# One function set on ScalarE, a scaling of the value weights, and a new share-out of the opening's PSUM copies in an FFT-plus-channel-mix kernel

## The chip, the cores and the metric

The kernel runs on 1 core of one Trainium2 chip. The metric is the device time of one execution in microseconds (us). The core's engines are TensorE (PE in the profile, with its weight loads as PEld), VectorE (DVE), ScalarE (ACT), GpSimd (POOL) and SyncE (SP). Each engine works through its own list of instructions in the order in which they were recorded; semaphores order the engines against each other.

## The reference

```python
X = fft(fft(x, axis=1), axis=2).real               # x: 8 x 3072 x 256, float32
x_prev = X shifted by one along the sequence, zeros first
xk = mu_k * X + (1 - mu_k) * x_prev
xr = mu_r * X + (1 - mu_r) * x_prev
k  = max(xk @ w_k, 0)                              # w_k: 256 x 1024
v  = (k * k) @ w_v                                 # w_v: 1024 x 256
r  = 1 / (1 + exp(-(xr @ w_r)))                    # w_r: 256 x 256
out = r * v
```

## The kernel before, in words

The program is one straight list, written out in Python; the order of the recording calls is the order on every engine, and it is pinned. It has an **opening**, in which tables are made and the transform of batch 0 is worked out in pieces, and then a loop over 192 steps (8 batches x 6 chunks of 512 positions x 4 steps).

PSUM holds three wide buffers of 1024 columns (`ps_w()`, psW) and two of 512 (`ps_v()`, psV), each given out in turn. A buffer that is given out again waits for the engines that read it before. Where ScalarE and VectorE both read one buffer, the program also keeps the two one behind the other.

The transform of a batch has three stages on TensorE. Stage one (`a_sum`, L681) multiplies the folded input `p` (made on VectorE by `fold`, L172 and L174) with `w_pm`; its result is copied to `a`. Stage two (`d_units`, L703) makes 13 units of 256 columns, copied to `g_all` by `d_evac`; `d_small` is the same for one or two units in a psV buffer. One column of each unit is then turned by a small product (`turned`, L752). Stage three (`c_sums`, L771) sums `f = 0` and `f = 1` parts into "slots" of 128 columns; they are copied to `y`. All these copies go through `evac`: ScalarE at L574, VectorE at L572.

The mix makes `x` from `y`: `diff` (L854) takes differences `d`, `scaled` (L866) multiplies with mu, `mixed` (L877) adds. The first four slots of batch 0 are mixed apart, by `ts` (L308: any tensor-scalar operation) and a scalar_tensor_tensor at L1049 that reads its other operand from the PSUM buffer named `first`.

A step of the loop (`k_piece`) multiplies `x` with a quarter of `w_k` into a psW buffer (L912), and ScalarE takes the relu of it into `rl` (L922), with a scale of 0.25. `square` (L932) squares a piece on VectorE. The value products (`v_part`, L965, for the first chunks, `v_tile`, L953, later) follow three to five steps behind. `r_item` makes the products with `w_r` (L939) and the sigmoid (L944), and `v_out` (L975) multiplies value and sigmoid on VectorE and writes the result out.

What a step does besides is in a table: `at(step, f, ...)` puts a call into a step, either among the TensorE products ("x") or behind them ("w"); `event(step, ...)` puts it between the two. Within a step the order is `k_piece`, "x", value products, "e", "w", the output, and last the square. The first two pieces of the first chunk are multiplied in two halves of 256 columns: the first half belongs to slots 0 to 3 and stands in the opening, the second half in steps 0 and 1.

`keep_busy(n, ps)` (L235) records n products of zeros whose results nobody reads; `NF` holds the counts by place. Names with a number behind them (psW_360, x_388) are buffers by the number of their allocation, which differs between the two programs; `first` is psW_361 in both.

Of the kernel before, what the change touches and what calls it, by code (L numbers as in the profile page):

```python
# [39 lines left out]
def kernel(  # L40
# [37 lines left out]
    def ps_w():  # L78
        return ps_slot("W", 3, 1024)
# [152 lines left out]
    def keep_busy(n, ps, cols=512):  # L232

        for _ in range(n):
            nc.tensor.matmul(out=ps[:, 0:cols], lhsT=zeros,  # L235
                             rhs=_v(zeros, 0, [(0, cols // P), (1, P)]), start=True, stop=True)

    fill = ps_w()
    keep_busy(4, fill)
    NF = (8, 4, 1, 3, 0, 0, 0)  # L240

# [58 lines left out]

    m_cs = const.tile([P, 3, NJ, 64], FP16)
    warm = const.tile([P, 1], FP32)
    nc.scalar.activation(out=warm, in_=zeros[:, 0:1], func=AF.Sin, bias=0.0, scale=1.0)
    def ts(out, in0, s1, op0, s2=None, op1=None):
        kw = {} if op1 is None else {"op1": op1}
        V.tensor_scalar(out=out, in0=in0, scalar1=s1, scalar2=s2, op0=op0, **kw)  # L308
# [360 lines left out]
    def a_sum(b, h, i0, eng="A", m=4):  # L669


        if (h, i0) == (0, 0):
            a_tile(b)
        ps = ps_w() if m == 4 else ps_v()
        for i in range(m):
            parts = [(h, i0 + i + 1 - h, 0, 2 * WA, 0, 1)]
            if h and i0 + i == 7:
                parts = [(0, 0, 0, WA, WA, 1), (1, 7, 1, WA, 1, 2)]
            for half, q, o, n, w, step in parts:
                for k in range(2):  # L680
                    nc.tensor.matmul(out=_v(ps, 256 * i + o, [(2 * WA // n, n)]),  # L681
                                     lhsT=p_t[b, half][0:96, q, 128 * k:128 * k + 128],
                                     rhs=_v(w_pm[0:96], (WA + WB) * k + w,
                                            [(WA + WB, 2), (step, n // 2)]),
                                     start=(k == 0), stop=(k == 1))
        a_ps[b, h, i0] = ps
        if eng:
            a_evac(b, h, i0, eng, m)
# [7 lines left out]
    def d_units(b, ps, u0, n, bank):  # L696

        for i in range(n):  # L700
            for e in range(2):
                o = bank * e + 128 * i
                nc.tensor.matmul(out=ps[:, o:o + 128],  # L703
                                 lhsT=a_t[b][:, e, 2 * (u0 + i):2 * (u0 + i) + 2, :],
                                 rhs=w_eo[:, e], start=True, stop=True)
# [228 lines left out]
    def r_item(c):  # L934
        b, m, i = c
        ps = ps_w()
        for tb in range(4):
            for a in range(2):
                nc.tensor.matmul(out=ps[:, 256 * tb:256 * tb + 256],  # L939
                                 lhsT=x_t[b, 1, m][:, a, 512 * i + 128 * tb:  # L940
                                                   512 * i + 128 * tb + 128],
                                 rhs=wr_sb[m][a], start=(a == 0), stop=(a == 1))
        st["r", c] = o_pool.tile([P, 1024], FP16, name="r", bufs=2)
        nc.scalar.activation(out=st["r", c], in_=ps, func=AF.Sigmoid)  # L944

    def v_tile(c, tb):

# [21 lines left out]
    def v_out(c, tb, n):  # L969
        b, m, i = c  # L970
        o = o_pool.tile([P, 2, 256], FP32, name="o" if n == 2 else f"o{tb}",
                        bufs=4 if n == 2 else 1)
        t0 = tb + 1 - n

        V.scalar_tensor_tensor(out=o.rearrange("p a b -> p (a b)")[:, 0:256 * n],  # L975
                               in0=st["v", t0][:, 0:256 * n], scalar=16.0,
                               in1=st["r", c][:, 256 * t0:256 * (t0 + n)],
                               op0=ALU.mult, op1=ALU.mult)
# [14 lines left out]
    eo_rest()  # L993
    m_sine(0, NJ1)
    m_sine(NJ1, NJ)
    nc.scalar.activation(out=warm, in_=zeros[:, 0:1], func=AF.Sigmoid)
    fold(0, 0, 1, 4)
    mu_ps = ps_v()
    for a in range(2):
# [2 lines left out]
    for n in range(2):  # L1002
        outer(mu_ps[:, 4 + n:5 + n], (tv(TO + n, 0, (1, P)), rv(ONE, 0, (1, 1))))
    keep_busy(NF[1], fill)
    a_sum(0, 0, 0)
    fold(0, 0, 5, 4)
    a_sum(0, 0, 4)
    nc.scalar.activation(out=muf_t, in_=mu_ps[:, 0:6], func=AF.Copy)
    loads()
    keep_busy(NF[2], ang_ps[1])  # L1010
    fold(0, 1, 0, 4)
    a_sum(0, 1, 0, "A")
    fold(0, 1, 4, 4)
# [1 line left out]
    a_sum(0, 1, 4, "V", 2)  # L1015
    a_sum(0, 1, 6, "A", 2)
    turn_table()
    nc.scalar.activation(out=mu_n, in_=mu_f, func=AF.Copy, bias=1.0, scale=-1.0)
    m_neg()
    fill = ps_w()  # L1020
    keep_busy(NF[3], fill)
    small = [ps_v(), ps_v()]
    for u, ps in enumerate(small):
        d_units(0, ps, u, 1, 128)
        d_evac(ps, u, 1, 128, "AV"[u])
    d_units(0, fill, 2, 4, 512)
# [5 lines left out]
    turned(0, 2, small[0][:, 256:258], "V")  # L1032
    ts(g_0[:, 0:1], small[0][:, 256:257], -1.0, MUL)
# [9 lines left out]
    x_t[0, 0, 0] = mix_pool.tile([P, 2, 1536], FP16, name="x00")  # L1043
    for a in range(2):
        t = x_t["t", a] = mix_pool.tile([P, 24, 64], FP16, name=f"t{a}")
        ts(t[:, 0:4], y[:, 0:4, a], mu_n[:, a, 0:1], MUL)
    for a in range(2):
        for z in range(2):
            V.scalar_tensor_tensor(out=_v(x_t[0, 0, 0], 1536 * a + 64 * z, [(128, 2), (1, 64)]),  # L1049
                                   in0=_v(first, 512 + 64 * a - 384 * z, [(128, 2), (1, 64)]),  # L1050
                                   scalar=mu_f[:, a, 0:1],
                                   in1=_v(x_t["t", a], 64 * z, [(128, 2), (1, 64)]),
                                   op0=ALU.mult, op1=ALU.add)
    odd = ps_v()
    even = ps_v()
    for f in range(2):
        c_sums((w[:, 0:512], w[:, 512:1024]), 5, 4, f)
    keep_busy(NF[5], w[:, 768:1024], 256)
    turned(4, 8, fill[:, 0:4])
    c_sums((even, odd), 9, 8, 0)  # L1060
    keep_busy(NF[6], w[:, 768:1024], 256)
    c_sums((even, odd), 9, 8, 1)
    y_evac(0, 5, 4, w)
    for z, p in enumerate((odd, even)):
        evac(_v(y, 128 * (9 + z), [(256, 4), (1, 128)]), p, "A")

    work = {}

# [33 lines left out]
    for a in range(2):  # L1104
        for ds in range(2):
            k_products(chunks[0], ds, 0, 256, (a,))
# [138 lines left out]
    for step in range(nk + LAG):  # L1245
        if step < nk:
            k_piece(chunks[step // 4], step % 4)
        due(step, "x")
        v = v_steps.get(step)
        if v and step not in early_v:  # L1250
            v_tile(*v)
        if step in p_steps and step not in early_v:
            v_part(*p_steps[step])
        due(step, "e")
        if step + 1 in early_v:
            if step + 1 in v_steps:
                v_tile(*v_steps[step + 1])
            if step + 1 in p_steps:
                v_part(*p_steps[step + 1])
        early = step in OUT_FIRST  # L1260
        for v in o_steps.get(step, ()) if early else ():
            v_out(*v)
        due(step, "w")
        for v in () if early else o_steps.get(step, ()):
            v_out(*v)
        if step < 4 * EARLY + 4:
            square(chunks[step // 4], step % 4, 1, step in SQUARE_A)
        elif step < nk and step % 2:
            square(chunks[step // 4], step % 4)
# [32 lines left out]
```

## Time and profile before

| | |
|---|---|
| median of 3 runs | 426.31 us (426.04 to 426.9) |
| the profiled execution | 426.17 us, of which the span from the first to the last instruction is 424.4 us |
| TensorE busy | 418.4 us (99%), 3974 products |
| VectorE busy | 371.3 us (87%) |
| ScalarE busy | 332.4 us (78%) |
| GpSimd busy | 64.2 us (15%) |
| HBM | 32.08 MB read, 25.17 MB written |

In the rows of the trace the first number is the start in us from the first instruction and the second is the duration; "x8" means that eight instructions were merged into one row, whose duration then runs from the first start to the last end. What stands in brackets is the idle time of the engine before it and what ended it. In the groups by shape the columns behind the bar are the busy time in us, the mean of one in ns, and the idle time before them. Instructions of one engine overlap a little in the rows (the next starts some 0.1 us before the last has ended), so a chain of them is added up from start to start.

### The profile page before, as it was taken

What the parts mean: (1) busy time and instruction counts of PE and PEld (TensorE: products, weight loads), DVE (VectorE), ACT (ScalarE), POOL (GpSimd) and SP (SyncE); (2) the same over time, 40 slices, a digit from 0 to 9 for tenths busy, and PEclk for the clock granted to TensorE, in tenths of its full rate; (3) what the DMA queues carried; (4) which work ended last, traced back from release to release, by engine and by line L of the source; (5) the groups of instructions that cost most, each with busy time, mean ns of one, the idle gap of its engine ahead of it and who ended that gap; (6) DMA issues with size and microseconds to landing.
All of it is one profiled execution on the core that took longest, in us unless ns stands there. A gap on an engine that the chain in (4) does not pass through costs nothing.

```text
span 424.4 us, 9646 instructions
## 1 busy us (share of the span) xinstructions
PE 418.4 (99%) x3974; PEld 294.1 (69%) x3974; DVE 371.3 (87%) x593; ACT 332.4 (78%) x438; POOL 64.2 (15%) x99
## 2 busy tenths in 40 slices
PE   8999999999999999999999999999999999999996
PEld 3767766776677767776767776777777776776765
DVE  8899999999898999989999899989999676977553
ACT  7889886798768986699767996689876997666661
POOL 7478500200060001400041000500000000000000
PEclk9999999999999999999999999999999999999999
DMA  8779962632385223932349232772233232332333
GB/s 171 111 111 195 224 156 57 113 91 64 70 151 147 64 59 62 215 101 51 76 77 220 52 75 59 134 174 55 52 76 72 58 73 52 74 74 51 76 76 99
DMA packets 35104, 42.08 MB, mean 99 GB/s; under 512 B 4114, under 2 KB 31092, under 8 KB 35060
## 3 DMA queue, kind: packets, MB, share of 16 engines
q1 hardware_dynamic: 27488, 25.41, 24.4%
q0 software_dynamic: 7264, 15.80, 21.8%
q8 instruction: 31, 0.51, 0.5%
q10 hardware_dynamic: 308, 0.26, 0.2%
q14 instruction: 13, 0.11, 0.1%
HBM read 32.08 MB, written 25.17 MB: 135 GB/s over the span
## 4 chain that ended last, share of the span: by engine, by line
PE 98%; DVE 1%; issue 0%; POOL 0%; ACT 0%; POOLq 0%
PE psW L912 39%; PE psV L953 37%; PE psW L939 10%; PE psV L965 3%; PE psW L611 3%; PE psW L235 1%; PE psV L611 1%; PE psW L681 1%; PE psW L703 1%; PE psV L378 1%; PE psW L771 0%; PE psW L803 0%; DVE rw L308 0%; PE psV L703 0%; PE psW L663 0%
## 5 line engine op out<-in xcount | busy, mean ns | idle before, releaser
L922 ACT ACTIVATE rl<-psW 128x1024 f16<-128x1024 f32 x192 | 194.3, 1039 | 79.2 <-PE psW L912 75.5
L912 PE MATMUL psW<-x,wk 128*128 128x512 f16 (+1 forms) x776 | 194.4, 377 | 0.3 <-DVE x L1049 0.3
L953 PE MATMUL psV<-wv_sb,k 128*128 128x256 f16 x1424 | 184.2, 273 | 0.0
L953 PEld LDWEIGHTS <-k 128*128 128x128 f16 x1424 | 136.8, 98 | 38.9
L932 DVE TENSOR_TENSOR k<-rl 128x2048 f16<-128x2048 f16 (+1 forms) x100 | 115.5, 1156 | 32.9 <-ACT rl L922 32.8
L912 PEld LDWEIGHTS <-wk 128*128 128x128 f16 x776 | 75.7, 98 | 53.7 <-issue 0.4
L975 DVE SCALAR_TENSOR_TENSOR o<-psV,r 128x512 f32<-128x512 f32 (+1 forms) x97 | 65.7, 680 | 10.0 <-PE psV L953 9.0
L877 DVE TENSOR_TENSOR x<-y,t 128x1536 f16<-128x1536 f16 (+3 forms) x76 | 62.4, 827 | 2.2
L944 ACT ACTIVATE r<-psW 128x1024 f16<-128x1024 f32 x48 | 50.0, 1043 | 0.8 <-PE psW L939 0.8
L939 PE MATMUL psW<-wr,x 128*128 128x256 f16 x384 | 49.8, 273 | 0.0
L939 PEld LDWEIGHTS <-x 128*128 128x128 f16 x384 | 37.5, 98 | 14.1
L574 ACT ACTIVATE a<-psW 128x832 f16<-128x832 f32 (+4 forms) x36 | 29.0, 851 | 0.2 <-PE psW L663 0.2
L574 ACT ACTIVATE g_all<-psW 128x512 f16<-128x512 f32 (+5 forms) x47 | 26.7, 646 | 0.3 <-PE psW L703 0.2
L494 POOL IOTA gate<- 1x1 int32 x7 | 0.8, 121 | 163.4 <-DVE gate L493 163.4
L141 POOL DMA_INDIRECT xm<-in_x_dram,idx_g x18 | 23.3, 1294 | 5.5 <-issue 5.5
L866 DVE TENSOR_SCALAR t<-d,muf_t 128x1536 f16<-128x1536 f16 (+3 forms) x44 | 21.9, 508 | 0.1
L172 DVE TENSOR_TENSOR p<-xp,xm 112x2304 f16<-112x2304 f16 (+6 forms) x19 | 21.6, 1139 | 0.0
L574 ACT ACTIVATE pq<-psW 128x1024 f16<-128x1024 f32 (+1 forms) x21 | 20.4, 1007 | 0.1
L866 DVE TENSOR_SCALAR t<-d,mu_m 128x1536 f16<-128x1536 f16 x32 | 19.6, 611 | 0.0
L854 DVE TENSOR_TENSOR d<-y 128x1664 f16<-128x1664 f16 (+5 forms) x19 | 16.7, 879 | 0.3 <-ACT y L574 0.3
L846 DVE TENSOR_TENSOR y<-pq 128x960 f16<-128x960 f16 (+3 forms) x28 | 15.7, 603 | 0.4
L965 PE MATMUL psV<-wv_sb,k 128*128 128x256 f16 x112 | 14.7, 273 | 0.0
(158 smaller groups left out, 236.3 us busy)
## 6 DMA issues: line engine op xcount, KB each, us to landing
out_dram<-o SPq DMA_DIRECT2D x189, 128.0 KB, 2.4
xp<-in_x_dram POOLq DMA_DIRECT2D x12, 216.0 KB, 5.2
xp<-in_x_dram POOLq DMA_DIRECT2D x13, 192.0 KB, 6.8
xp<-in_x_dram POOLq DMA_DIRECT2D x2, 384.0 KB
wv_sb<-in_moe_w_v_dram POOLq DMA_DIRECT2D x1, 512.0 KB
xp<-in_x_dram SPq DMA_DIRECT2D x1, 480.0 KB, 4.3
xp<-in_x_dram POOLq DMA_DIRECT2D x1, 432.0 KB, 4.9
xm<-in_x_dram,idx_g POOLq DMA_INDIRECT x18, 6.9
```

The lines of the kernel that those rows point to most:

```text
L141: nc.gpsimd.indirect_dma_start(dst, None, src, bass.IndirectOffsetOnAxis(ap=idx, axis=0))
L574: nc.scalar.activation(out=out_ap, in_=in_ap, func=AF.Copy)
L866: V.tensor_scalar(out=dst, in0=src, scalar1=mu, scalar2=None, op0=ALU.mult)
L877: V.tensor_tensor(out=_v(x_t[b, j, m], o, [(64 * step, hi - lo), (step, 64)]), in0=y_t[b][:, lo + 3 * m:hi + 3 * m, a], in1=x_t["t", a][:, ...
L912: nc.tensor.matmul(out=st["k", ds][:, 512 * hs + lo:512 * hs + hi], lhsT=wk_sb[m][a][:, 128 * fc:128 * fc + 128], rhs=xk[:, a, 512 * i + l ...
L922: nc.scalar.activation(out=st["rl"][:, 2 * ds:2 * ds + 2], in_=st["k", ds].rearrange("p (f t) -> p f t", f=2), func=AF.Relu, bias=0.0, sca ...
L932: V.tensor_tensor(out=k2_t[c][:, lo:hi], in0=r, in1=r, op=ALU.mult)
L939: nc.tensor.matmul(out=ps[:, 256 * tb:256 * tb + 256], lhsT=x_t[b, 1, m][:, a, 512 * i + 128 * tb: 512 * i + 128 * tb + 128], rhs=wr_sb[m] ...
L944: nc.scalar.activation(out=st["r", c], in_=ps, func=AF.Sigmoid)
L953: nc.tensor.matmul(out=st["v", tb - h][:, 256 * h:256 * h + 256], lhsT=k2_t[c][:, fc, 128 * tb:128 * tb + 128], rhs=wv_sb[:, fc], start=(f ...
L965: nc.tensor.matmul(out=st["v", tb - h][:, 256 * h:256 * h + 256], lhsT=k2_t[c][:, fc, 128 * tb:128 * tb + 128], rhs=wv_sb[:, fc], start=fc ...
L975: V.scalar_tensor_tensor(out=o.rearrange("p a b -> p (a b)")[:, 0:256 * n], in0=st["v", t0][:, 0:256 * n], scalar=16.0, in1=st["r", c][:, ...
```

## The change: what it does

1. **Sigmoid from tanh.** `r` becomes tanh(0.5 z) instead of sigmoid(z), and `v_out` computes (r + 1) * v; the factor 1/2 and the former factor 16 are put into the value weights, which are multiplied by 8 in place, once, by VectorE. `r` is stored in float32 instead of float16. ScalarE loads one function set, at the start; the second load and the dummy activation behind it are gone.
2. **First four slots.** The multiplication with `mu_n`, which read the copied `y`, now reads the PSUM buffer `first`, so those four slots no longer wait for the copy to `y`, and the copy itself comes later.
3. **The opening.** Stage two's units 6 and 7 go into the second halves of the two psV buffers instead of a psW buffer; stage three is summed for slots 0 to 3 and 4 to 8 instead of 0 to 4 and 5 to 8; its last part (`c_sums((even, odd), 9, 8, 1)`) comes behind the first two products with `w_k`. The copies are shared out anew between ScalarE and VectorE. Three places with zero products remain, with 8, 2 and 2 of them (before: 8, 4, 1 and 3). The copies of mu to `muf_t` and `mu_n` come ahead of stage one's.
4. **The first square** comes ahead of the rest of step 0, and the scaling of the value weights right behind it.

The diff, cut to these:

```diff
-    NF = (8, 4, 1, 3, 0, 0, 0)
+    NF = (8, 2, 2)
...
-    nc.scalar.activation(out=warm, in_=zeros[:, 0:1], func=AF.Sin, bias=0.0, scale=1.0)
+    nc.scalar.activation(out=warm, in_=zeros[:, 0:1], func=AF.Silu)
...
-        st["r", c] = o_pool.tile([P, 1024], FP16, name="r", bufs=2)
-        nc.scalar.activation(out=st["r", c], in_=ps, func=AF.Sigmoid)
+        st["r", c] = o_pool.tile([P, 1024], FP32, name="r", bufs=2)
+        nc.scalar.activation(out=st["r", c], in_=ps, func=AF.Tanh, scale=0.5)
...
-                               in0=st["v", t0][:, 0:256 * n], scalar=16.0,
-                               in1=st["r", c][:, 256 * t0:256 * (t0 + n)],
-                               op0=ALU.mult, op1=ALU.mult)
+                               in0=st["r", c][:, 256 * t0:256 * (t0 + n)], scalar=1.0,
+                               in1=st["v", t0][:, 0:256 * n], op0=ALU.add, op1=ALU.mult)
...
-    nc.scalar.activation(out=warm, in_=zeros[:, 0:1], func=AF.Sigmoid)
...
-    d_units(0, w[:, 256:1024], 6, 2, 512)
-    V.tensor_copy(out=g_0[:, 1:128], in_=g_all[:, 0, 129:256])
+    for u, ps in enumerate(small):
+        d_units(0, ps[:, 256:512], 6 + u, 1, 128)
...
-    d_evac(w[:, 256:1024], 6, 2, 512, "V")
-    c_sums((first[:, 0:512], first[:, 512:1024]), 0, 5, 0)
-    c_sums((first[:, 0:512], first[:, 512:1024]), 0, 5, 1)
-    turned(2, 4, small[1][:, 256:258], "V")
-    d_evac(fill[:, 256:1024], 4, 1, 512, "A")
-    d_evac(fill[:, 384:1024], 5, 1, 512, "V")
-    y = y_t[0]
-    y_evac(0, 0, 4, first)
-    evac(y[:, 4].rearrange("p a t -> p (a t)"), first[:, 256:384], "A")
+    c_sums((first[:, 0:512], first[:, 512:1024]), 0, 5, 0)
+    turned(2, 4, small[0][:, 2:4], "")
+    c_sums((w[:, 0:512], w[:, 512:1024]), 4, 5, 0)
+    c_sums((first[:, 0:512], first[:, 512:1024]), 0, 5, 1)
+    d_evac(fill[:, 256:1024], 4, 2, 512, "A")
+    d_evac(small[0][:, 256:512], 6, 1, 128, "A")
+    d_evac(small[1][:, 256:512], 7, 1, 128, "V")
+    evac(_v(g_all, 256 * 2 + 128, [(256, 2)]), small[0][:, 2:4], "V")
+    c_sums((w[:, 0:512], w[:, 512:1024]), 4, 5, 1)
...
-        ts(t[:, 0:4], y[:, 0:4, a], mu_n[:, a, 0:1], MUL)
-    for a in range(2):
+        ts(_v(t, 0, pairs), _v(first, 64 * a, [(512, 2), (128, 2), (1, 64)]), mu_n[:, a, 0:1], MUL)
...
+    def k_first(*parts):
+        for ds, a in parts:
+            k_products(chunks[0], ds, 0, 256, (a,))
...
+    k_first((0, 0))
+    c_sums((even, odd), 9, 8, 1)
+    for z, p in enumerate((odd, even)):
+        evac(_v(y, 128 * (9 + z), [(256, 4), (1, 128)]), p, "A")
+    k_first((1, 0), (0, 1), (1, 1))
+    y_evac(0, 0, 4, first)
...
+    at(0, ts, wv_sb, wv_sb, 8.0, MUL)
+    event(0, (square, chunks[0], 0, 1))
...
-        if step < 4 * EARLY + 4:
+        if 0 < step < 4 * EARLY + 4:
```

The order on VectorE around step 0, before; k is the square, the CAST copies the unit of `d_small(0, 12, 1)` out of its psV buffer, and x, t and d are the mix of slots 8 to 15:

```order
L854 TENSOR_TENSOR d<-y 128x1024
L866 TENSOR_SCALAR t_470<-d,muf_t 128x512
L866 TENSOR_SCALAR t_472<-d,muf_t 128x512
L877 TENSOR_TENSOR x_388<-y,t_470 128x512
L877 TENSOR_TENSOR x_388<-y,t_472 128x512
L932 TENSOR_TENSOR k_463<-rl 128x1024
L572 CAST g_all<-psV_482 128x2x2x64
```

The same place now:

```order
L854 TENSOR_TENSOR d<-y 128x1024
L932 TENSOR_TENSOR k_460<-rl 128x1024
L308 TENSOR_SCALAR wv_sb<-wv_sb 128x2048
L866 TENSOR_SCALAR t_469<-d,muf_t 128x512
L866 TENSOR_SCALAR t_471<-d,muf_t 128x512
L877 TENSOR_TENSOR x_391<-y,t_469 128x512
L877 TENSOR_TENSOR x_391<-y,t_471 128x512
L572 CAST g_all<-psV_480 128x2x2x64
```

The square moved ahead of four mix operations, the scaling of the value weights is new between them, and the copy out of the psV buffer stands behind all of it.

The order on ScalarE from stage two's first copies to the first relu (rl), before:

```order
L574 ACTIVATE g_all<-psV_343 128x2x2x64
L574 ACTIVATE g_all<-psW_339 128x2x4x64
L574 ACTIVATE g_all<-psW_339 128x2x2x64
L574 ACTIVATE y<-psW_361 128x512
L574 ACTIVATE y<-psW_361 128x128
L574 ACTIVATE g_all<-psW_339 128x4
L574 ACTIVATE y<-psW_360 128x512
L574 ACTIVATE y<-psV_397 128x4x128
L574 ACTIVATE y<-psV_398 128x4x128
L574 ACTIVATE g_all<-psV_438 128x2x4x64
L574 ACTIVATE g_all<-psV_456 128x2x4x64
L922 ACTIVATE rl<-psW_428 128x1024
```

And now:

```order
L574 ACTIVATE g_all<-psV_338 128x2x2x64
L574 ACTIVATE g_all<-psW_335 128x2x4x64 x2
L574 ACTIVATE g_all<-psV_338 128x2x2x64
L574 ACTIVATE g_all<-psW_335 128x4
L574 ACTIVATE y<-psW_360 128x512
L574 ACTIVATE y<-psW_360 128x128
L574 ACTIVATE y<-psV_402 128x4x128
L574 ACTIVATE y<-psV_403 128x4x128
L574 ACTIVATE y<-psW_361 128x512
L574 ACTIVATE g_all<-psV_435 128x2x4x64
L574 ACTIVATE g_all<-psV_453 128x2x4x64
L922 ACTIVATE rl<-psW_414 128x1024
```

The copy of `first` (psW_361) moved from ahead of the two psV copies of `y` to behind them, and between the psV copies and the first relu there are now three copies instead of two.

More of the change, by code (lines that the diff above doesn't have):

```diff
@@ L1004 @@
     keep_busy(NF[1], fill)
+    nc.scalar.activation(out=muf_t, in_=mu_ps[:, 0:6], func=AF.Copy)
+    nc.scalar.activation(out=mu_n, in_=mu_f, func=AF.Copy, bias=1.0, scale=-1.0)
     a_sum(0, 0, 0)
@@ L1007 @@
     a_sum(0, 0, 4)
-    nc.scalar.activation(out=muf_t, in_=mu_ps[:, 0:6], func=AF.Copy)
     loads()
-    keep_busy(NF[2], ang_ps[1])
     fold(0, 1, 0, 4)
@@ L1017 @@
     turn_table()
-    nc.scalar.activation(out=mu_n, in_=mu_f, func=AF.Copy, bias=1.0, scale=-1.0)
     m_neg()
     fill = ps_w()
-    keep_busy(NF[3], fill)
+    keep_busy(NF[2], fill)
     small = [ps_v(), ps_v()]
@@ L1025 @@
         d_evac(ps, u, 1, 128, "AV"[u])
+    V.tensor_copy(out=g_0[:, 1:128], in_=g_all[:, 0, 129:256])
     d_units(0, fill, 2, 4, 512)
     d_evac(fill, 2, 2, 512, "A")
+    for u, ps in enumerate(small):
+        d_units(0, ps[:, 256:512], 6 + u, 1, 128)
     w, first = ps_w(), ps_w()
-    d_units(0, w[:, 256:1024], 6, 2, 512)
-    V.tensor_copy(out=g_0[:, 1:128], in_=g_all[:, 0, 129:256])
     c_tiles(0)
-    turned(0, 2, small[0][:, 256:258], "V")
-    ts(g_0[:, 0:1], small[0][:, 256:257], -1.0, MUL)
@@ L1045 @@
         t = x_t["t", a] = mix_pool.tile([P, 24, 64], FP16, name=f"t{a}")
-        ts(t[:, 0:4], y[:, 0:4, a], mu_n[:, a, 0:1], MUL)
-    for a in range(2):
+        ts(_v(t, 0, pairs), _v(first, 64 * a, [(512, 2), (128, 2), (1, 64)]), mu_n[:, a, 0:1], MUL)
         for z in range(2):
[L1049 to L1052, printed above, removed]
+            V.scalar_tensor_tensor(out=_v(x_t[0, 0, 0], 1536 * a + 64 * z, pairs[1:]),
+                                   in0=_v(first, 512 + 64 * a - 384 * z, pairs[1:]),
+                                   scalar=mu_f[:, a, 0:1], in1=_v(t, 64 * z, pairs[1:]),
@@ L1053 @@
                                    op0=ALU.mult, op1=ALU.add)
+    turned(4, 8, fill[:, 0:4])
     odd = ps_v()
     even = ps_v()
[L1056 to L1059, printed above, removed]
     c_sums((even, odd), 9, 8, 0)
[L1061 to L1065, printed above, removed]
+    y_evac(0, 4, 4, w)
```

8 lines of the change are left out of this document (5 added, 3 removed).

## The prediction

> **What bounds the kernel now.** I read the page first: the busy shares, the clock, the chain, and the two lines with the most products.
>
> ```profile
> span 424.4 us, 9646 instructions
> PE 418.4 (99%) x3974; PEld 294.1 (69%) x3974; DVE 371.3 (87%) x593; ACT 332.4 (78%) x438; POOL 64.2 (15%) x99
> PE 98%; DVE 1%; issue 0%; POOL 0%; ACT 0%; POOLq 0%
> L912 PE MATMUL psW<-x,wk 128*128 128x512 f16 (+1 forms) x776 | 194.4, 377 | 0.3 <-DVE x L1049 0.3
> L953 PE MATMUL psV<-wv_sb,k 128*128 128x256 f16 x1424 | 184.2, 273 | 0.0
> ```
>
> TensorE is 98% of the chain and the products of the two large lines waited 0.3 us in all. Then the windows, to see where TensorE is not full:
>
> ```profile
> 14.00:20.00 6.00, 5.48 (x75) 3.85 (x73) 5.42 (x23) 4.88 (x13) 0.54 (x2) 1.00 0.92 129
> 20.00:23.00 3.00, 3.00 (x22) 1.88 (x22) 2.96 (x8) 3.00 (x5) 2.18 (x3) 1.00 0.17 22
> 30.00:420.00 390.00, 390.00 (x3745) 276.76 (x3743) 343.55 (x480) 307.23 (x385) 45.03 (x58) 1.00 0.45 97
> ```
>
> The columns are the stretch, its length, and the busy time of PE, PEld, DVE, ACT and POOL, then the clock. From 20 us on TensorE has no gap: 3.00 of 3.00, 390.00 of 390.00. The work behind that point is the same in both programs, so the change can win or lose only by when TensorE gets onto this gapless stretch and whether it stays there. Everything hangs on the opening, and the timeline of TensorE shows its last part:
>
> ```profile
> 12.03 0.38 PE L235 MATMUL psV<-zeros 128*128 128x512 f16 x1
> 12.25 0.88 PE L681 MATMUL psW<-w_pm,p 96*128 96x208 f16 x8
> 17.22 0.74 PE L771 MATMUL psV<-m_cs,g_all 64*128 64x128 f16 x16
> 18.25 1.03 PE L912 MATMUL psW<-x,wk 128*128 128x256 f16 x8 [0.29 <-DVE x L1049]
> 22.52 1.04 PE L965 MATMUL psV<-wv_sb,k 128*128 128x256 f16 x8
> ```
>
> Eight products of 256 columns are 0.11 us apart ((1.03 - 0.27)/7), so the fifth value product of L965 starts at 22.52 + 4 x 0.11 = 22.96. That one is the point that I follow.
>
> **The change part by part.** ScalarE and VectorE in the opening:
>
> ```profile
> 10.11 1.28 ACT L996 ACT_TABLE_LOAD   x1
> 11.52 1.62 ACT L574 ACTIVATE a<-psW 128x832 f16<-128x832 f32 x2
> 14.05 0.55 ACT L574 ACTIVATE a<-psV 128x416 f16<-128x416 f32 x1
> 15.54 0.87 ACT L574 ACTIVATE g_all<-psW 128x512 f16<-128x512 f32 x2 [0.17 <-PE psW L703]
> L574 ACT ACTIVATE g_all<-psW 128x256 f16<-128x256 f32 x1 | 0.4, 378 | 0.0
> 18.00 1.08 ACT L574 ACTIVATE y<-psV 128x512 f16<-128x512 f32 x2
> 19.54 1.09 ACT L574 ACTIVATE g_all<-psV 128x512 f16<-128x512 f32 x2 [0.46 <-PE psV L703]
> 20.51 3.78 ACT L922 ACTIVATE rl<-psW 128x1024 f16<-128x1024 f32 x4
> L922 ACT ACTIVATE rl<-psW 128x1024 f16<-128x1024 f32 x4 | 3.8, 1052 | 0.0
> 13.04 0.16 DVE L174 TENSOR_TENSOR p<-xp,xm 96x1 f16<-96x1 f32 x1
> 16.57 0.17 DVE L572 CAST g_all<-psV 128x2 f16<-128x2 f32 x1
> 16.65 0.41 DVE L572 CAST g_all<-psW 128x256 f16<-128x256 f32 x1
> 17.09 0.48 DVE L308 TENSOR_SCALAR t<-y,mu_n 128x256 f16<-128x256 f16 x2
> 17.49 1.13 DVE L1049 SCALAR_TENSOR_TENSOR x<-psW,muf_t,t 128x128 f16<-128x128 f32 x4
> 19.79 0.69 DVE L854 TENSOR_TENSOR d<-y 128x1024 f16<-128x1024 f16 x1
> 20.52 0.62 DVE L866 TENSOR_SCALAR t<-d,muf_t 128x512 f16<-128x512 f16 x2
> 21.05 0.76 DVE L877 TENSOR_TENSOR x<-y,t 128x512 f16<-128x512 f16 x2
> 21.72 0.70 DVE L932 TENSOR_TENSOR k<-rl 128x1024 f16<-128x1024 f16 x1
> 22.35 0.41 DVE L572 CAST g_all<-psV 128x256 f16<-128x256 f32 x1
> ```
>
> *Table load and zero products.* The load takes 1.28 us off ScalarE, but the copy behind it (11.52) needs stage one, which needs the folds, and the last fold ends at 13.04 + 0.16 = 13.20 in both programs. Of the four zero products that go, only the one inside stage one lies on the path: 12.25 - 12.03 = 0.22. So the last copy of stage one starts at 13.83 instead of 14.05, and everything behind it is 0.22 earlier, as far as nothing else comes in between. The load itself is worth nothing; if the folds were no cover, its 1.28 would be the most.
>
> *Stage two's copies.* The first copy of `fill` comes at 15.54 - 0.22 = 15.32. ScalarE now copies four units of it, twice 0.60 long and 0.49 apart (19.54 to 20.51 holds two such), and then unit 6 (0.38): 15.32 + 0.98 + 0.38 = 16.68. Unit 6 lies in the same psV buffer as the turned columns of units 2 and 3, and VectorE's copy of these waits until ScalarE is through: 16.72.
>
> *First slots from PSUM.* The multiplication with `mu_n` starts one small copy later (0.08, as 16.57 to 16.65): 16.80. No row shows a tensor-scalar of 256 columns out of PSUM; a copy of that shape takes 0.41, and
>
> ```profile
> 7.14 0.73 DVE L308 TENSOR_SCALAR rl<-psV,ph_c 128x512 int32<-128x512 f32 x1
> ```
>
> one of twice the columns 0.73. I take 0.46, near the copy, where two out of SBUF took 0.48 together. The Trainium skill, in "VectorE: DVE Perf Modes", section "Why PSUM operands drop a tier", says that a float32 operand in PSUM holds VectorE at its slowest rate, which speaks against this edit; its table ("The TRN2 errata") gives 120 + 256 cycles at 0.96 GHz, an estimate of 0.39, and the sum would be 0.07 smaller by it. Of the two L1049 operations of a half, 0.26 apart and 0.34 long (four in 1.13), the second ends at 16.80 + 0.46 + 0.04 + 0.60 = 17.90; before, 17.49 + 0.60 = 18.09. The other half ends at 18.92, before at 17.49 + 1.13 = 18.62. The first half is 0.2 earlier, the second 0.3 later.
>
> *Last part of stage three.* The first two products with `w_k` start 0.16 behind the half, as before (18.09 to 18.25): 18.06. Two of them take 0.22, and then come the eight products of stage three, half of the 0.74 row plus the end of the last, about 0.4: 18.68. ScalarE's copies of the two psV buffers to `y`, at 18.00 before, start at 18.70. Here the change costs: TensorE was waiting anyway, but ScalarE has these two, the copy of `first` and the two of `d_small` ahead of the first relu: five at 0.485 are 2.43, so the relu starts at 21.13 instead of 20.51, and ends 1.05 later at 22.18 (21.56).
>
> *VectorE in step 0.* Slots 4 to 8 and the differences end at about 20.8 (0.3 later than 20.48). Before, VectorE went on with the four mix operations; now the square stands ahead of them and waits for the relu, and VectorE is idle for 1.4. Queued behind that wait are the scaling, the mix, and the copy out of the psV buffer into which TensorE puts its fifth value product. From the end of the relu: 0.04, the square 0.63 (21.72 to 22.35), the scaling, the mix 1.20 (20.52 to 21.72), the copy 0.41. For the scaling (2048 columns of float16 in SBUF) the nearest rows are
>
> ```profile
> L866 DVE TENSOR_SCALAR t<-d,mu_m 128x1536 f16<-128x1536 f16 x32 | 19.6, 611 | 0.0
> 7.91 0.71 DVE L308 TENSOR_SCALAR rl<-rl 128x1024 int32<-128x1024 int32 x1
> ```
>
> 0.61 for three quarters of it, and 0.71 for half in another type, so between 0.61 and about 1.3; I take 0.75, near the first, of which 0.67 stands start to start. Sum: 22.18 + 0.04 + 0.63 + 0.67 + 1.20 + 0.41 = 25.13, where the copy ended at 22.76 before. TensorE starts the fifth value product at 25.18 instead of 22.96: **2.2 us later**. Its other waits lie inside this one: the fourth piece of the first chunk waits for the first relu's buffer (0.2), and the first value product for the scaled weights, at 23.6 instead of 22.52.
>
> *Afterwards* TensorE has its old list and no slack, so the 2.2 stay. The tanh costs nothing that I can see:
>
> ```profile
> L944 ACT ACTIVATE r<-psW 128x1024 f16<-128x1024 f32 x48 | 50.0, 1043 | 0.8 <-PE psW L939 0.8
> L975 DVE SCALAR_TENSOR_TENSOR o<-psV,r 128x512 f32<-128x512 f32 (+1 forms) x97 | 65.7, 680 | 10.0 <-PE psV L953 9.0
> ```
>
> Storing `r` in float32 could lengthen 48 operations and reading it 97; at 0.1 each that is 4.8 and 9.7 us on engines that are 78% and 87% busy, and VectorE waited 10.0 for TensorE at this very line. A gain there would be just as hidden. The cover is TensorE's own list; without it they would cost those amounts.
>
> **The rivals.** *The opening's 0.22 comes through, and VectorE's new order holds nobody up.* That is the other side: not slower, 426.1 for the execution. It decides itself at the copy out of psV: it must end by 22.7, so the first relu by 19.75 (2.95 earlier). For it: stage one does end earlier, and the first mix half too. Against it: five copies of 0.485 stand ahead of the relu, behind products that need the first mix half.
>
> *The relu is on time for the square.* If ScalarE gets through by 20.8, VectorE does not idle, and only its 0.3 of lateness and the scaling (0.67) are left: +1.0, 427.3. It needs the copies to start at 17.3 (20.8 - 1.05 - 2.43), ahead of the first mix half at 17.90 on which their products wait by the sum above.
>
> *The clock falls.* With the gaps TensorE may be throttled again. At the start of the program
>
> ```profile
> 6.07 3.14 PE L235 MATMUL psW<-zeros 128*128 128x512 f16 x8
> 20.79 1.89 PE L912 MATMUL psW<-x,wk 128*128 128x512 f16 x8
> ```
>
> eight zero products of 512 columns took 3.14 us, where eight of that width took 1.89 later. One more such slow stretch of 3.14 us would add 1.25 to the 2.2: 429.8. The windows above show 1.00 through the gaps of 0.5 us between 14 and 20; the longest that I expect is 1.1. The Trainium skill's "TensorE: Matmul & The Clock Gate", section "Part 1: The HAM clock gate", has the clock halve only after an idle window of about 3.4 us; by that the rival has no ground, and no row here shows a gap of such length.
>
> **How the numbers follow.** The profiled execution took 426.17, 1.8 more than its span, and 0.14 less than the median of 426.31. The forecast is 426.31 + 2.2 = 428.5. Chances: forecast 0.73, relu on time 0.12, opening comes through 0.11, clock 0.04. The range goes from the second case (426.31 + 1.0 = 427.3) to the forecast with its upper costs: the scaling at 1.3 adds 0.55 and the PSUM operation at 0.73 adds 0.27, 2.2 + 0.8 = 3.0, rounded up by 0.1 for the scatter of the runs: 429.4. At the lower bounds (0.61 and 0.41) it is 428.3, inside. What a measurement of this kernel can tell from no change is about 0.2%, 0.85 us. Not slower by my mechanism is 0.2 us, so most of that case counts as the same (0.06) and a part as faster, if the earlier opening brings more than I see (0.05); of the second case 0.04 falls within 0.85. Slower: 0.73 + 0.08 + 0.04 = 0.85.
>
> **What would show it.** In the profile after: no second table load; the last fold at 13.2; the first L1048 half ending near 17.9; the copies of the psV buffers to `y` starting near 18.7; the first relu at 21.1; VectorE idle for over 1 us in front of L932, released by ScalarE; a scaling of 0.75; TensorE idle for about 1.1 between the fourth and the fifth L965 product, released by a VectorE copy at L572; and 390.00 of 390.00 later on. I am wrong if the first relu ends before 20.8, if the fifth product doesn't wait, or if TensorE shows gaps behind 30 us.

## The result, and the profile after

The changed kernel takes **428.72 us** (median of 6 runs, 428.4 to 429.15), against 426.31 for the kernel before (6 runs as well): 2.4 us slower, ratio 1.0056 with a 95% interval of 1.0043 to 1.0068. The forecast was 428.5, range 427.3 to 429.4. The profiled execution took 428.91 with a span of 427.1, 2.7 more than before. In the experiments below, one execution of the kernel without the scaling took 1536 us and is not counted in its ratio.

The page of the changed kernel: the span, the busy times, the chain and the group of the value products.

```profile
span 427.1 us, 9642 instructions
PE 418.9 (98%) x3972; PEld 293.4 (69%) x3972; DVE 371.8 (87%) x593; ACT 331.5 (78%) x437; POOL 63.6 (15%) x99
PE 90%; DVE 6%; ACT 2%; issue 1%; POOL 0%; DVEq 0%; POOLq 0%
L965 PE MATMUL psV<-wv_sb,k 128*128 128x256 f16 x112 | 14.9, 273 | 1.2 <-DVE g_all L572 0.9
```

The last of these groups in the kernel before:

```profile
L965 PE MATMUL psV<-wv_sb,k 128*128 128x256 f16 x112 | 14.7, 273 | 0.0
```

TensorE is busy as long as before (418.9 against 418.4); of the chain it has 90% where it had 98%, and VectorE has 6% instead of 1%. L965, which had no wait, now waited 1.2 us, 0.9 of it for a VectorE copy. The windows, with the columns as before, show where TensorE is empty:

```profile
14.00:20.00 6.00, 4.69 (x69) 3.26 (x68) 4.62 (x17) 4.16 (x11) 0.47 (x1) 1.00 0.86 116
20.00:26.00 6.00, 4.50 (x36) 2.75 (x33) 4.51 (x15) 5.38 (x8) 2.30 (x4) 1.00 0.21 28
30.00:420.00 390.00, 389.92 (x3741) 275.96 (x3739) 344.81 (x487) 309.61 (x389) 46.57 (x65) 1.00 0.45 97
```

The kernel before, from 23 us on (its stretch from 20 to 23 stands in the prediction):

```profile
23.00:30.00 7.00, 7.00 (x69) 4.66 (x67) 6.69 (x20) 5.61 (x9) 5.51 (x11) 1.00 0.78 114
```

From 14 to 20 us TensorE was busy 4.69 where it had been 5.48, and from 20 to 26 it has a hole of 1.5 where there was none. Behind 30 us it is all but full, at a clock of 1.00. VectorE's timeline through the place:

```profile
20.48 0.69 DVE L854 TENSOR_TENSOR d<-y 128x1024 f16<-128x1024 f16 x1
22.66 0.69 DVE L932 TENSOR_TENSOR k<-rl 128x1024 f16<-128x1024 f16 x1 [1.49 <-ACT rl L922]
23.27 0.69 DVE L308 TENSOR_SCALAR wv_sb<-wv_sb 128x2048 f16<-128x2048 f16 x1
23.87 0.61 DVE L866 TENSOR_SCALAR t<-d,muf_t 128x512 f16<-128x512 f16 x2
24.40 0.75 DVE L877 TENSOR_TENSOR x<-y,t 128x512 f16<-128x512 f16 x2
25.07 0.41 DVE L572 CAST g_all<-psV 128x256 f16<-128x256 f32 x1
```

ScalarE, and then TensorE, in stage one and at the same place:

```profile
12.69 1.62 ACT L574 ACTIVATE a<-psW 128x832 f16<-128x832 f32 x2 [0.54 <-PE psW L681]
14.19 0.56 ACT L574 ACTIVATE a<-psV 128x416 f16<-128x416 f32 x1
19.16 1.08 ACT L574 ACTIVATE y<-psV 128x512 f16<-128x512 f32 x2 [0.59 <-PE psV L771]
21.56 2.90 ACT L922 ACTIVATE rl<-psW 128x1024 f16<-128x1024 f32 x3
10.90 1.14 PE L681 MATMUL psW<-w_pm,p 96*128 96x208 f16 x10
24.01 0.60 PE L965 MATMUL psV<-wv_sb,k 128*128 128x256 f16 x4 [0.31 <-DVE wv_sb L308]
25.54 0.60 PE L965 MATMUL psV<-wv_sb,k 128*128 128x256 f16 x4 [0.93 <-DVE g_all L572]
```

Read from the end: the fifth value product starts at 25.54 (22.96 before), released by the copy at 25.07 to 25.48; that copy follows the mix, the scaling and the square, and the square waited 1.49 us for the first relu, while VectorE did nothing. The 2.58 of this one point are nearly all of the 2.7 of the span.

One row does not belong to the change: ScalarE's second copy of stage one (12.69) came after 0.54 of idling although the row of its products ends at 12.04 (10.90 + 1.14), and so the last one is at 14.19. In nine of the ten kernels below the copies show no such pause; in one it lies at the third copy, whose products are late there. It makes everything behind it in this one execution about 0.35 later (14.19 against 13.84 for the last copy in the first experiment); without it the fifth product would be at about 25.19.

### The profile page after: what moved, and what is told of

The parts are those of the page before. It is cut to its first block, busy times and chain, and to the rows that moved or that the text cites. A ratio compares the mean times of both kernels' runs of the same rounds, so it can differ in the third digit from the quotient of the medians.

```text
span 427.1 us, 9642 instructions
## 1 busy us (share of the span) xinstructions
PE 418.9 (98%) x3972; PEld 293.4 (69%) x3972; DVE 371.8 (87%) x593; ACT 331.5 (78%) x437; POOL 63.6 (15%) x99
## 4 chain that ended last, share of the span: by engine, by line
PE 90%; DVE 6%; ACT 2%; issue 1%; POOL 0%; DVEq 0%; POOLq 0%
PE psV L953 37%; PE psW L912 36%; PE psW L939 9%; PE psW L611 3%; DVE x L877 1%; DVE t L866 1%; DVE k L932 1%; DVE o L975 1%; PE psV L611 1%; PE psW L235 1%; PE psV L965 1%; DVE p L172 1%; ACT y L574 1%; PE psV L378 1%; ACT g_all L574 1%
## 5 line engine op out<-in xcount | busy, mean ns | idle before, releaser
L975 DVE SCALAR_TENSOR_TENSOR o<-r,psV 128x512 f32<-128x512 f32 (+1 forms) x97 | 65.3, 676 | 9.4 <-PE psV L953 8.9
L944 ACT ACTIVATE r<-psW 128x1024 f32<-128x1024 f32 x48 | 50.1, 1044 | 0.8 <-PE psW L939 0.8
L965 PE MATMUL psV<-wv_sb,k 128*128 128x256 f16 x112 | 14.9, 273 | 1.2 <-DVE g_all L572 0.9
```

The costliest lines, as they stand in the source:

```text
L944: nc.scalar.activation(out=st["r", c], in_=ps, func=AF.Tanh, scale=0.5)
```

## The experiments

Times are medians; the ratio is against the kernel before on the same chip (426.03 us for the first four, 426.2 for the next four, 426.6 for the last two), with its 95% interval. The ratio is worked out from the single executions and is not exactly the quotient of two medians. Kernels from different chips are compared by their ratios; a ratio of 0.0001 is 0.043 us.

**The first square at the end of step 0 again** (ratio 1.0026, 1.0017 to 1.0035; 427.21 us). The edit, on the changed kernel:

```diff
-    event(0, (square, chunks[0], 0, 1))
-        if 0 < step < 4 * EARLY + 4:
+        if step < 4 * EARLY + 4:
```

> The changed kernel with the first square at the end of step 0 again; everything else, the scaling too, stays. Theory (the order on VectorE behind the relu sets the fifth value product): VectorE does the scaling and the mix while ScalarE is still at the relu, so 21.17 + 0.67 + 1.20 = 23.04 for the mix, square to 23.67, the psV copy to 24.08, the fifth value product at 24.13 instead of 25.54: 1.4 us faster than the changed kernel, about 427.3. Rival (the late relu itself is what costs, in whatever order VectorE works): under 0.3 us from the changed kernel, 428.5. Rival (the gaps or the clock): no change, 428.7.

Its timeline, ScalarE, VectorE and TensorE:

```profile
13.84 0.55 ACT L574 ACTIVATE a<-psV 128x416 f16<-128x416 f32 x1
18.80 1.08 ACT L574 ACTIVATE y<-psV 128x512 f16<-128x512 f32 x2 [0.59 <-PE psV L771]
21.20 1.99 ACT L922 ACTIVATE rl<-psW 128x1024 f16<-128x1024 f32 x2
21.00 0.69 DVE L308 TENSOR_SCALAR wv_sb<-wv_sb 128x2048 f16<-128x2048 f16 x1 [0.19 <-DMA wv_sb<-in_moe_w_v_dram]
22.84 0.68 DVE L932 TENSOR_TENSOR k<-rl 128x1024 f16<-128x1024 f16 x1
23.57 1.05 PE L965 MATMUL psV<-wv_sb,k 128*128 128x256 f16 x8 [0.22 <-DVE k L932]
```

The eight value products run in one piece again, the fifth at 24.01: 1.3 us of the 2.4 (0.0056 - 0.0026 in the ratio; in the traces 25.19 without the pause against 24.01) came from the order alone. Both rivals, which expected under 0.3 or nothing from it, fall. The rest is the late relu (21.20) and the scaling, which pushes the mix, and with it the square, to 22.84. The scaling also waits 0.19 for the weights themselves to land.

**The scaling ahead of the square** (ratio 1.0039, 1.0026 to 1.0053; 427.79 us).

```diff
-    at(0, ts, wv_sb, wv_sb, 8.0, MUL)
+    event(0, (ts, wv_sb, wv_sb, 8.0, MUL))
     event(0, (square, chunks[0], 0, 1))
```

> The changed kernel with the scaling of the value weights ahead of the first square instead of behind it; the same operations. Theory: the scaling falls into VectorE's idle 1.49 us in front of the square and leaves the queue behind it, so the psV copy and the fifth value product come 0.69 earlier: 24.85 instead of 25.54, about 428.05. Rival (the scaling is hidden where it is, and the mix alone decides): no change, 428.7. If the weights have not landed by 21.2 us, the square comes later and the kernel is slower.

VectorE and TensorE:

```profile
20.95 0.69 DVE L308 TENSOR_SCALAR wv_sb<-wv_sb 128x2048 f16<-128x2048 f16 x1
22.31 0.69 DVE L932 TENSOR_TENSOR k<-rl 128x1024 f16<-128x1024 f16 x1 [0.67 <-ACT rl L922]
24.59 0.60 PE L965 MATMUL psV<-wv_sb,k 128*128 128x256 f16 x4 [0.80 <-DVE g_all L572]
```

VectorE's idle time shrinks to 0.67 and the fifth product comes at 24.59; take off the 0.35 that only the other execution lost, and 0.6 are the scaling. The ratio falls by 0.0017 (0.7 us); the two intervals overlap, so the size rests on the trace. The scaling stood in the queue that TensorE waited for, as the theory says.

**The tanh by itself** (ratio 1.0002, 0.9993 to 1.0011; 426.16 us): the kernel before with one function set, the tanh and the float32 `r`, and the factor 8 in the relu's scale, so that nothing is scaled on VectorE.

```diff
-                             func=AF.Relu, bias=0.0, scale=0.25)
+                             func=AF.Relu, bias=0.0, scale=math.sqrt(0.5))
...
+        nc.scalar.activation(out=st["r", c], in_=ps, func=AF.Tanh, scale=0.5)
```

> The kernel before with part 1 alone: one function set, tanh, r in float32, and the factor 8 in the relu's scale (0.7071 for 0.25, squared 8 times as much) instead of in the weights, so no scaling on VectorE. Theory: the table load and the dummy activation were hidden, the tanh and the float32 r lie behind TensorE: 426.3, within 0.2. Rival (the set switch was worth something): up to 1.3 us faster, 425.0. Rival (the wider r costs VectorE or ScalarE time that TensorE waits for): over 0.4 us slower.

Two groups of one shape each, of this kernel:

```profile
L975 DVE SCALAR_TENSOR_TENSOR o<-r,psV 128x512 f32<-128x512 f32 x95 | 64.6, 683 | 9.2 <-PE psV L953 8.4 <-PE psV L965 0.5
L944 ACT ACTIVATE r<-psW 128x1024 f32<-128x1024 f32 x48 | 50.1, 1044 | 0.8 <-PE psW L939 0.8
```

One output operation takes 683 ns (685 in the same view of before) and one tanh 1044 (the sigmoid 1043). No difference that can be told: the load that goes was hidden in this opening, and the wider `r` costs neither engine anything that shows. Both rivals, 1.3 us faster or over 0.4 slower, fall.

**The square first in the kernel before** (ratio 1.0024, 1.0015 to 1.0033; 427.2 us).

```diff
+    event(0, (square, chunks[0], 0, 1))
     at(0, mix_part, 0, 0, 8, 16)
-        if step < 4 * EARLY + 4:
+        if 0 < step < 4 * EARLY + 4:
```

> The kernel before with one edit: the first square ahead of the rest of step 0. Theory: the relu ends at 21.56, the square runs to 22.23, the mix to 23.43, the psV copy to 23.84, the fifth value product starts at 23.88 instead of 22.96: 0.9 us slower than before, about 427.2. Rival (the order is harmless and it is the later opening that costs): no change, 426.3.

VectorE and TensorE:

```profile
21.47 0.69 DVE L932 TENSOR_TENSOR k<-rl 128x1024 f16<-128x1024 f16 x1 [1.09 <-ACT rl L922]
23.74 0.60 PE L965 MATMUL psV<-wv_sb,k 128*128 128x256 f16 x4 [0.73 <-DVE g_all L572]
```

The same edit in the other kernel does the same: VectorE waits 1.09 for the relu, TensorE 0.73 for the copy, the fifth product is 0.78 later than in the profiled execution of before, and the time is 1.0 longer (0.9 expected). This opening is the one of the kernel before, unchanged, but in this execution it ran 0.11 earlier (the first value product starts at 22.41, against 22.52), so its own order delays the fifth product by 0.89. Behind it there is one more pause, which the first experiment's execution has as well. From the waits around 53 us:

```profile
PE psW L703 <- DVE g_all L572: 0.3, 1, 0.3
```

There TensorE waits for a buffer that VectorE empties late. The products there start about 0.47 further apart than in before (1.03 instead of 0.56) in these two executions. Other executions have less: 0.42 with VectorE's copy ahead of ScalarE's, 0.25 with the best parts together, 0.24 in the changed kernel, and none with the scaling ahead of the square or with unit 12 copied by ScalarE. So the pause does not follow the order in step 0, and its cause stays open.

**Without the scaling** (ratio 1.0013, 1.0003 to 1.0022; 426.83 us): the first experiment's kernel, with the factor 8 in the relu.

```diff
-    at(0, ts, wv_sb, wv_sb, 8.0, MUL)
...
+                             func=AF.Relu, bias=0.0, scale=math.sqrt(0.5))
```

> The changed kernel with the first square at the end of step 0 again, and without the scaling of the weights: the factor 8 goes into the relu's scale (0.7071 for 0.25). What is left of the change is the tanh and the opening. Theory: the mix now ends at 22.05 and the square begins when the first relu is through, at 22.31; the first value product starts at 23.03 instead of 22.52, so the late relu still costs 0.5: about 426.5 on the chip of the first four (0.5 above before, 0.6 below the kernel with only the square put back). Rival (the scaling was all that was left of the loss once the square is back): as before, 426.0. Rival (the mid-kernel gap of 0.47 near 53 us is what is left): as with the square put back, 427.2.

VectorE, then TensorE:

```profile
22.32 0.69 DVE L932 TENSOR_TENSOR k<-rl 128x1024 f16<-128x1024 f16 x1 [0.17 <-ACT rl L922]
22.33 1.02 PE L912 MATMUL psW<-x,wk 128*128 128x512 f16 x4 [0.15 <-ACT rl L922]
23.19 1.04 PE L965 MATMUL psV<-wv_sb,k 128*128 128x256 f16 x8
```

Now VectorE waits for the relu only 0.17, and what is left of the loss, 0.6, is put down to the relu: the fourth piece waits for its buffer, so the first value product comes at 23.19 (23.03 expected; 22.52 before). Both rivals fall: the time is neither that of before nor that of the first experiment. Without the scaling the ratio is 0.0013 (0.55 us) lower, though the scaling stood in the time of the relu in the first experiment. In the trace the value products are 0.38 earlier (23.19 against 23.57); the first experiment's execution also has 0.38 more of the pause near 53 us, which may or may not belong to the scaling.

**The last part of stage three ahead of the first `w_k` products** (ratio 1.0007, 0.9998 to 1.0016; 426.54 us): the kernel without the scaling, with

```diff
-    k_first((0, 0))
     c_sums((even, odd), 9, 8, 1)
+    k_first((0, 0))
```

> The kernel without the scaling (square last, factor in the relu), and the last part of stage three again ahead of the first two products with w_k. Theory: ScalarE's copies of the psV buffers begin at about 18.2 instead of 18.8, and the relu, then held by the products of its second half, at 20.85 instead of 21.2; the first value product 0.35 earlier, about 426.2, level with before within 0.2. Rival (the relu is late for the copies of unit 6 and the first mix half, not for this order): no change against the kernel without the scaling, 426.5.

ScalarE, then TensorE:

```profile
18.08 1.11 ACT L574 ACTIVATE y<-psV 128x512 f16<-128x512 f32 x2
20.83 1.95 ACT L922 ACTIVATE rl<-psW 128x1024 f16<-128x1024 f32 x2
22.86 1.04 PE L965 MATMUL psV<-wv_sb,k 128*128 128x256 f16 x8
```

The copies begin 0.7 earlier, the relu 0.38, the value products 0.33. In the trace this edit is half of the relu's lateness; the two medians, from one chip, differ by 0.3. The intervals of the ratios overlap, but nine of these eleven executions are below the fastest of the other kernel (426.68).

**The opening alone, with the table load back** (ratio 1.0021, 1.0012 to 1.003; 427.1 us): the kernel without the scaling, with sigmoid, float16 `r`, the factors of before, and

```diff
     m_sine(NJ1, NJ)
+    nc.scalar.activation(out=warm, in_=zeros[:, 0:1], func=AF.Sigmoid)
```

> The kernel without the scaling (square last), with the sigmoid, the float16 r and the second table load put back: the change's opening alone. Theory, refined: the load was hidden in the kernel before because the mu copies stood behind stage one's first two copies; with the mu copies ahead, the first copy of stage one comes at 11.83 instead of 11.27 and the last at 14.19 instead of 13.84, so 0.35 more than the kernel without the scaling, about 426.9. Rival (the load is hidden here as well): the same as that kernel, 426.5.

ScalarE here, and then in the kernel without the scaling:

```profile
10.10 1.28 ACT L996 ACT_TABLE_LOAD   x1
11.81 2.35 ACT L574 ACTIVATE a<-psW 128x832 f16<-128x832 f32 x3
14.04 0.56 ACT L574 ACTIVATE a<-psV 128x416 f16<-128x416 f32 x1
```

```profile
11.27 2.47 ACT L574 ACTIVATE a<-psW 128x832 f16<-128x832 f32 x3 [0.88 <-PE psW L681]
13.85 0.55 ACT L574 ACTIVATE a<-psV 128x416 f16<-128x416 f32 x1
```

With the copies of mu ahead of stage one's, the load is no longer free: the first copy is 0.54 late and the last 0.19 (0.35 expected). Of the difference, 0.12 goes among the three copies (2.47 becomes 2.35), and 0.23 in front of the last one, which began 0.11 after the third had ended and now begins 0.12 before. The medians differ by 0.27; the intervals of the ratios overlap, but the executions themselves hardly do (426.68 to 427.04 without the load, 427.0 and more with it).

The Trainium skill's "ScalarE: Activation LUTs", section "Rules for kernel authors", budgets about 2.7 us for each switch to another set. This case does not agree: the next activation follows the 1.28 us of the load at once (10.10 + 1.28, 11.40). By the page's figure, an estimate, the first copy would have been 1.4 later still.

**The best parts together** (ratio 0.9995, 0.9986 to 1.0004; 426.0 us): the kernel with the tanh alone, the mu copies ahead of stage one and fewer zero products.

```diff
-    NF = (8, 4, 1, 3, 0, 0, 0)
+    NF = (8, 2, 0, 2, 0, 0, 0)
...
     keep_busy(NF[1], fill)
+    nc.scalar.activation(out=muf_t, in_=mu_ps[:, 0:6], func=AF.Copy)
+    nc.scalar.activation(out=mu_n, in_=mu_f, func=AF.Copy, bias=1.0, scale=-1.0)
```

> The kernel before with the tanh (factor in the relu's scale, no second table load), the copies of mu ahead of stage one's and two zero products inside stage one fewer; the rest of the opening and step 0 as before. Theory: the last copy of stage one starts at 13.84 instead of 14.05, and nothing behind it is disturbed, so the opening's 0.2 comes through: 0.2 faster than before, about 425.85, at the edge of what can be told. Rival (VectorE, not TensorE's products, sets the opening): no change.

ScalarE, then TensorE:

```profile
13.89 0.55 ACT L574 ACTIVATE a<-psV 128x416 f16<-128x416 f32 x1
22.34 0.82 PE L965 MATMUL psV<-wv_sb,k 128*128 128x256 f16 x6
```

The value products start at 22.34 instead of 22.52. But the kernel with the tanh alone, whose opening has neither of these two moves, is nearly as early:

```profile
22.37 0.82 PE L965 MATMUL psV<-wv_sb,k 128*128 128x256 f16 x6
```

Its last copy of stage one starts at 13.90, and with the load still in place (the square first in the kernel before) the two times are 13.95 and 22.41. So, with one execution of each, 0.11 of the 0.18 is the profiled execution of before, 0.04 goes with the tanh, and the mu copies and the zero products add 0.03. The time is 0.2 shorter, inside the interval: not told apart from before.

**VectorE's copy ahead of ScalarE's** (ratio 1.0004, 0.9995 to 1.0013; 426.68 us): the kernel with stage three first, with

```diff
-    c_sums((w[:, 0:512], w[:, 512:1024]), 4, 5, 0)
     c_sums((first[:, 0:512], first[:, 512:1024]), 0, 5, 1)
+    c_sums((w[:, 0:512], w[:, 512:1024]), 4, 5, 0)
...
-    d_evac(small[0][:, 256:512], 6, 1, 128, "A")
     d_evac(small[1][:, 256:512], 7, 1, 128, "V")
     evac(_v(g_all, 256 * 2 + 128, [(256, 2)]), small[0][:, 2:4], "V")
+    d_evac(small[0][:, 256:512], 6, 1, 128, "A")
```

> The kernel with the square last, no scaling and the last part of stage three ahead of the w_k products, with two more places put in another order: VectorE copies the turned columns of units 2 and 3 before ScalarE copies unit 6 out of the same psV buffer, and the f = 1 products of slots 0 to 3 come before the f = 0 products of slots 4 to 8. Theory (that copy and those products hold the first mix half): the first half of the mix begins at 16.52 instead of 16.80, the first w_k product and the relu come 0.28 earlier, 0.28 faster than without the two moves, about 426.25 where before is 426.2. Rival (the relu waits for ScalarE's five copies, whose start the moves don't change): no change, 426.55.

In the profiled execution, one of the slowest of its eleven, a fold on VectorE began after 0.54 us of idling, for which the trace names no cause, so stage two begins late. Rows of this kernel, then of the one without the two moves:

```profile
11.64 0.69 DVE L172 TENSOR_TENSOR p<-xp,xm 96x1024 f16<-96x1024 f16 x1 [0.54 <-issue]
15.21 0.40 PE L703 MATMUL psV<-w_eo,a 128*128 128x128 f16 x4 [0.21 <-DVE m_cs L308]
17.24 0.48 DVE L308 TENSOR_SCALAR t<-psW,mu_n 128x256 f16<-128x256 f32 x1
23.31 0.93 PE L965 MATMUL psV<-wv_sb,k 128*128 128x256 f16 x7
```

```profile
14.45 0.40 PE L703 MATMUL psV<-w_eo,a 128*128 128x128 f16 x4 [0.21 <-ACT a L574]
16.80 0.47 DVE L308 TENSOR_SCALAR t<-psW,mu_n 128x256 f16<-128x256 f32 x1
```

From the start of stage two the mix begins 2.03 later instead of 2.35, and the value products 8.10 instead of 8.41 (22.86 - 14.45): 0.32 and 0.31 earlier, where 0.28 was expected. This compares one execution of each, one of them with a late start, and the times don't resolve it.

**Unit 12 copied by ScalarE** (ratio 1.0031, 1.0018 to 1.0043; 428.06 us), in the changed kernel:

```diff
-    at(1, d_small, 0, 12, 1, "V")
+    at(1, d_small, 0, 12, 1, "A")
```

> The changed kernel, its order of step 0 and its scaling untouched, with one letter changed: ScalarE instead of VectorE copies unit 12 out of the psV buffer that the fifth value product takes. Theory (that copy, standing behind square, scaling and mix in VectorE's queue, is all that the fifth value product waits for): ScalarE does it behind the second relu at about 23.1 to 23.5, the fifth value product follows the fourth without a gap at 24.04 instead of 25.18 (25.54 in the profiled execution), 1.15 faster than the changed kernel, about 427.4. Rival (the mix or later squares are late as well and stop TensorE at the next place): under 0.5 faster, 428.2 or more.

The second square on VectorE, then TensorE:

```profile
25.07 0.68 DVE L932 TENSOR_TENSOR k<-rl 128x1024 f16<-128x1024 f16 x1
23.67 1.03 PE L965 MATMUL psV<-wv_sb,k 128*128 128x256 f16 x8 [0.31 <-DVE wv_sb L308]
25.81 1.05 PE L965 MATMUL psV<-wv_sb,k 128*128 128x256 f16 x8
27.78 0.59 PE L912 MATMUL psW<-x,wk 128*128 128x512 f16 x2 [0.37 <-DVE w_hh L538]
```

The eight value products are one piece and the fifth starts at 24.10, as worked out (24.04). In this execution TensorE then stops at what stands next in VectorE's queue: 0.23 for the second square, which ends at 25.75, 0.44 for the copy of the half tables, and 0.67 and 0.17 more near 42 us, where the trace names no releaser. This execution is the slowest of its six (428.81, the others 427.83 to 428.13), so not all of these stand in each. By the ratios the gain is 1.07 of the 1.15 expected; the medians are only 0.66 apart, but before takes 0.3 more on this chip. So the copy holds most of the loss, as the theory said. In the traced execution it is only the first thing that TensorE meets, and more of VectorE's queue is late behind the wait: the theory was too narrow for it.

## Why the prediction was right, point by point

The experiments' executions without the pause at 12.69 let the steps be read as they were worked out. The mechanism is the one forecast; in the first step the size is partly luck.

- *The last copy of stage one 0.22 earlier, at 13.83; the load and the folds as cover.* It starts at 13.84 (first experiment). But the 0.22 was read from one execution of before whose stage one began late (10.60). The same opening in the experiment with the square first in the kernel before began at 10.34, with the zero product still in place, and had its last copy at 13.95. Against that the gain is 0.11, and that the time of 13.83 was hit to 0.01 is luck. The load by itself was worth nothing in the old opening (1.0002). Only in the new opening would it have cost (0.19 in the trace), which I had not seen: there the mu copies that it delays stand ahead of stage one's.
- *The copy of the turned columns waits for ScalarE's unit 6 (16.72), and the product with `mu_n` starts at 16.80.* Both are at 16.72 and 16.80 in the kernel with stage three first. Taking that wait away and issuing the f = 1 products earlier brought 0.31 from the start of stage two.
- *The PSUM product at 0.46.* It took 0.47, and the copy of the same shape (0.41) was the near row. The estimate of 0.39 from the Trainium skill's "VectorE: DVE Perf Modes", section "The TRN2 errata", falls short by 0.08. The first mix half ended at 17.92 (17.90 worked out).
- *Copies to `y` from 18.70, relu from 21.13.* 18.80 and 21.20. Half of its lateness against before is the late part of stage three.
- *The square waits 1.4 us for the relu; scaling, mix and copy behind it.* 1.49, released by ScalarE. This order is the largest part: 1.3 us in the changed kernel, 1.0 in the kernel before. The scaling took 0.69 where I took 0.75 between 0.61 and 1.3. The Trainium skill's "VectorE: DVE Perf Modes", section "The perf-mode tier table (the rule you actually need)", has 693 ns for a tensor-scalar of 2048 bf16 elements, and the row of float16 agrees.
- *The fifth value product at 25.18, 2.2 later, and the 2.2 stay.* 25.54 in the profiled execution, of which 0.35 are the pause; the median is 2.4 longer. The remaining 0.2 may be the pause in part of the runs, the 0.24 near 54 us, or the 0.11 by which the profiled execution of before was late itself; which, the runs don't tell. That there would be no gap behind 30 us was slightly wrong, and it was one of the signs named: TensorE has 389.92 of 390.00 there, with a cause that stays open.
- *The tanh and the float32 `r` cost nothing.* Shown by the kernel with these alone, to within 0.1% (1.0002, 0.9993 to 1.0011).
- *The rivals.* Where VectorE's order is left as it was, 0.18 of the opening's 0.2 shows at the value products, most of it owed to the profiled execution of before, and the time cannot be told from before (0.9995). The relu was not on time. The clock stayed at 1.00 through the gaps between 20 and 26 us, the longest 0.93. The idle window of about 3.4 us that the Trainium skill states in "TensorE: Matmul & The Clock Gate", section "Part 1: The HAM clock gate", was not tried, since no gap came near it.

By ratios, the loss of 0.56% is made up of 0.30% for the square's place, 0.13% for the scaling even in a better place, and 0.13% for what the opening leaves, the later relu, of which the position of stage three's last part is about half. Each ratio is uncertain by about 0.1%, so the first share is clear of noise and the two smaller ones rest on the traces as much as on the times.

## What to carry to other kernels

On an engine that works through one list, as VectorE does here, an instruction that waits holds up all that stands behind it (the square's wait of 1.49 us): put what must wait behind the work that is ready, and ask of each moved instruction who waits for the ones it now blocks. A one-off operation is not free because its engine idles nearby; the scaling cost 0.7 us more behind the square than ahead of it, and leaving it out saved 0.55 even where the square came last, while the same factor in a scale that ScalarE applies anyway cost nothing that could be measured. And a load that is hidden in one order of an engine's list can be on the path in the next.

## What was not expected of the hardware

The 512 KB of value weights, issued by GpSimd at 12.6 us, land only at about 21 us: in the first experiment the scaling, next in VectorE's list, waited 0.19 for them and started at 21.00. With the scaling ahead of the square it started at 20.95, where the trace names no wait. From one execution to another the opening shifts by up to 0.8 us: once a fold began at 11.64 instead of about 11.0, with no cause in the trace, and once ScalarE's second copy started 0.64 after its products had ended (12.69 against 12.04). The cause of both pauses stays open.
